# Banded attention and a feed-forward layer on one core: block sums of W1 built by adding DMA transfers instead of GpSimd additions

## The chip, the cores and the metric

The kernel runs on one core of a Trainium2 chip. The metric is the device time of one execution in microseconds (us); the median of several executions is compared. The engines of the core are TensorE (PE, its weight loads on a queue of their own, PEld), VectorE (DVE), ScalarE (ACT), GpSimd (POOL) and SyncE (SP). Each takes its instructions in the order of the program. DMA transfers are issued by SP, by POOL and, in one place, by ACT.

## What is computed

Attention over 4 batches and 8 heads (768 tokens, head dimension 64), in which a token sees the first 8 tokens and the 96 latest, with a bias that falls linearly with the distance; its output, 3072 tokens of 512 numbers, goes through a feed-forward layer. All in float32, but the two weight matrices arrive as float64:

```
scores = q @ k.T / 8 - slope[head] * dist,  -1e9 where not kept
a      = softmax(scores);   x = a @ v            # 3072 x 512
h      = x @ w_in                                # 512 -> 2048
out    = maximum(0.01 * h, h) @ w_out            # 2048 -> 512
```

## The kernel before

**Products.** Each float32 operand is split in a high part (rounded by a cast) and a low part (the rest), and each product is three matmuls: high by high, high by low, low by high. So a tile of the hidden layer (`hidden`, L1028: 128 hidden features by 384 tokens, four blocks of the 512 inputs) is 12 matmuls of 384 columns, and its way back to 512 outputs for 128 tokens (`project`, L1054) is 3 matmuls of 512 columns.

**Stages.** (1) Up to about 48 us the first attention units run while W1 (`wih`, `wil`) and W2 (`woh`, `wol`) are loaded and converted from float64. (2) A main loop of 96 steps `j` treats 2304 tokens in six chunks of 384: a step is one `hidden` (`ffn1(j)`) and three `project` (`ffn2(j - 1)`). The rest of the attention is hung between steps in "visits" (`visit`, L425; the steps at which they come are the list `VISITS`): a visit finishes two units (`attn_v` needs the tile `vr`, which SP has loaded; L310 to L338), starts two others, and issues loads for later ones. Results for the last 768 tokens are stored by POOL to a DRAM tensor `xd` (L356). (3) The last 768 tokens are done by `strassen` (L609), a Strassen-Winograd scheme with 7 instead of 8 block products: 8 iterations `i` with two of the 16 blocks of 128 hidden features each.

**The last phase.** An iteration has seven `product`s (six matmuls of 384 columns, L616), with blocks a11, a12, a22 of W1 or with one of four sums s1 to s4 of its blocks as weights, and as moving operand blocks of x (b11, b21, b22) or sums of them (t1 to t4). Between the products stand the 12 `project`s of the iteration before (`second`, L650; `todo` and `behind_` deal them out); in i = 0 there are only the three of the last main-loop step. DVE adds the products up (`add`, L636 to L638: u2, u3, c22, c21, c12), and `halves` (L626 to L634) makes the leaky maximum (L631, DVE), the cast (L632, ACT) and the low part (L633, DVE). `put` (L641 to L646) copies a finished output bank (L644) and stores it (L646, tensor `out_dram`); all six copies share three buffers with the tag "kept".

**Its operands.** `make_sums(i)` (L531 to L544) forms s1 to s4 of iteration i by ten POOL additions of 128x256 (high and low parts each), one iteration ahead; `split_sum` (L546 to L550) splits them with a cast on ACT and a subtraction on DVE. The differences of x (`diff`, L519 to L522, 128x768) are on POOL too: d1 gives t1, d2 t2, d4 t4, d3 t3. They are split by `split_x` (L514 to L517). `prepare(n)` (L566) hangs the loads of b (from `xd`, by POOL, L512), the differences and the splits at steps 12 to 1 before the end of the main loop. The split of b22 and the one of s4 for i = 0 come inside iteration 0.

The order of the instructions on each engine is the program's order as written; `pin` keeps it.

Of the kernel before, what the change touches and what calls it, by code (L numbers as in the profile page):

```python
# [18 lines left out]
P = 128  # L19
# [3 lines left out]
PAIRS = 22  # L23
HT = 384
SUPER = 2 * HT // P
VISITS = [39, 42, 46, 49, 53, 56, 60, 63, 67, 70, 74, 77, 81, 84, 88]
# [25 lines left out]
def fast_path(ctx, tc, qp, kp, vp, wi, wo, nvec, weights, nmall, out, B, H, S):  # L52
# [59 lines left out]
    def conversion(p):  # L112

        m, f = pieces[p]
        dh, dl = ((wih[:, :, f * P:(f + 1) * P], wil[:, :, f * P:(f + 1) * P]), (woh[:, f, :], wol[:, f, :]))[m]
# [383 lines left out]
    late, here = {}, {}  # L499
# [19 lines left out]
    def diff(name, in0, in1):  # L519
        t = pools["mem"].tile([P, 2, HT], F32, tag="diff", name="diff", bufs=2)  # L520
        pin(nc.gpsimd.tensor_tensor(out=t, in0=value(in0), in1=value(in1), op=ALU.subtract))
        late[name] = t  # L522

    def block(n, f, m):
        return [weights[x][:, 2 * m:2 * m + 2, f * P:(f + 1) * P] for x in range(2)]
# [4 lines left out]

    def make_sums(i):  # L531

        if i >= NF // 2:
            return
        b = blocks_of(i)
        a11, a12, a21, a22 = ([x.bitcast(F32) for x in b[k]] for k in ("a11", "a12", "a21", "a22"))
        for k, *terms in (("s1", a21[0], (ALU.add, a22[0]), (ALU.add, a21[1]), (ALU.add, a22[1])),
                          ("s2", here["s1"], (ALU.subtract, a11[0]), (ALU.subtract, a11[1])),
                          ("s3", a11[0], (ALU.subtract, a21[0]), (ALU.add, a11[1]), (ALU.subtract, a21[1])),
                          ("s4", a12[0], (ALU.subtract, here["s2"]), (ALU.add, a12[1]))):  # L540
            acc_ = terms[0]
            for op, t in terms[1:]:
                pin(nc.gpsimd.tensor_tensor(out=here[k], in0=acc_, in1=t, op=op))  # L543
                acc_ = here[k]  # L544

    def split_sum(i, k):  # L546
        if i >= NF // 2:
            return
        pin(nc.scalar.copy(out=late[k][0], in_=here[k]))
        pin(nc.vector.tensor_tensor(out=late[k][1], in0=here[k], in1=late[k][0].bitcast(F32), op=ALU.subtract))  # L550
# [15 lines left out]
    def prepare(n):  # L566
# [6 lines left out]
        elif n == -8:  # L573
# [8 lines left out]
            for k in ("s1", "s2", "s3", "s4"):  # L582
                late[k] = [mem.tile([P, 2, P], F32R, name=k + x) for x in "hl"]
                here[k] = mem.tile([P, 2, P], F32, name=k)
            make_sums(0)
            diff("d1", "b12", "b11")
            band_holds(tc, fl, nvec, nmall)
        elif n == -7:
            band_holds_everywhere(tc, fl, pools["ps"].tile([P, HT], F32, tag="ps_p", name="ps_f")[0:1, 0:1], flag)
        elif n == -6:  # L590
            split_sum(0, "s2")
            split_sum(0, "s3")
        elif n == -5:
            split_sum(0, "s1")
            split_x("b11")
        elif n == -4:
            diff("d2", "b22", "d1")
            split_x("t1", late["d1"])
        elif n == -3:
            split_x("t2", late["d2"])  # L600
            diff("d4", "d2", "b21")
        elif n == -2:
            split_x("t4", late["d4"])
            diff("d3", "b22", "b12")
            split_x("b21")
        elif n == -1:
            split_x("t3", late["d3"])

    def strassen():  # L609
# [26 lines left out]
        def add(name, in0, ps, op=ALU.add):  # L636
            t = in0 if name is None else ffn.tile([P, HT], F32, name="t") if name == "t" else mem.tile([P, HT], F32, name=name)
            pin(nc.vector.tensor_tensor(out=t, in0=in0, in1=ps, op=op))  # L638
# [498 lines left out]
```

## Time and profile before

| | us |
|---|---|
| median of 3 runs (lowest, highest) | 646.83 (646.46, 649.41) |
| the profiled execution | 644.86 |
| its span in the trace | 643.3 |
| PE busy | 621.2 (97%) |
| DVE busy | 424.6 (66%) |
| ACT busy | 291.4 (45%) |
| POOL busy | 119.5 (19%) |

The span runs from the first to the last instruction that the profiler saw; the execution's own time is 1.56 us longer. The table of windows among the rows below says how busy each engine was in a stretch of the span and is the place to look for idle time of PE. In the timelines a bracket behind an instruction says how long its engine had been idle ahead of it and what it waited for. The page's matmuls overlap: a matmul is shown for 0.34 or 0.40 us though the next starts sooner, so lost time is read from start to start.

### The profile page before, as it was taken

What the parts mean: (1) busy time and instruction counts of PE and PEld (TensorE: products, weight loads), DVE (VectorE), ACT (ScalarE), POOL (GpSimd) and SP (SyncE); (2) the same over time, 40 slices, a digit from 0 to 9 for tenths busy, and PEclk for the clock granted to TensorE, in tenths of its full rate; (3) what the DMA queues carried; (4) which work ended last, traced back from release to release, by engine and by line L of the source; (5) the groups of instructions that cost most, each with busy time, mean ns of one, the idle gap of its engine ahead of it and who ended that gap; (6) DMA issues with size and microseconds to landing.
All of it is one profiled execution on the core that took longest, in us unless ns stands there. A gap on an engine that the chain in (4) does not pass through costs nothing. (4 is left out here: it accounts for less than half of the span.)

```text
span 643.3 us, 14742 instructions
## 1 busy us (share of the span) xinstructions
PE 621.2 (97%) x5692; PEld 546.9 (85%) x5692; DVE 424.6 (66%) x1187; ACT 291.4 (45%) x822; POOL 119.5 (19%) x155
## 2 busy tenths in 40 slices
PE   5699999999999999999999999999999999999996
PEld 4588898898888888888888888898889878888885
DVE  6988998896667466575756566666227875555643
ACT  6977764545443344454434354445223532222212
POOL 3213300000000000000010020000145765555400
PEclk9899999999999999999999999999999999999999
DMA  8976743413667335376565666665620000000002
GB/s 275 355 269 217 224 153 132 142 55 120 220 202 242 107 112 185 123 230 199 187 183 180 225 208 196 212 225 184 182 66 1 26 25 1 2 1 0 2 1 102
DMA packets 56669, 92.79 MB, mean 144 GB/s; under 512 B 10144, under 2 KB 30688, under 8 KB 56592
## 3 DMA queue, kind: packets, MB, share of 16 engines
q1 hardware_dynamic: 54944, 86.79, 41.3%
q0 software_dynamic: 1504, 4.72, 2.4%
q8 instruction: 47, 0.77, 0.5%
q14 instruction: 30, 0.25, 0.1%
q10 hardware_dynamic: 144, 0.26, 0.1%
HBM read 70.26 MB, written 21.50 MB: 143 GB/s over the span
## 5 line engine op out<-in xcount | busy, mean ns | idle before, releaser
L1060 PE MATMUL ps_o<-woh,gl 128*128 128x512 f32 x336 | 133.3, 397 | 0.1
L1037 PE MATMUL ps_h<-xh,wih 128*128 128x384 f32 x384 | 132.8, 346 | 0.1
L1058 PE MATMUL ps_o<-woh,gh 128*128 128x512 f32 x336 | 132.4, 394 | 0.2
L1059 PE MATMUL ps_o<-wol,gh 128*128 128x512 f32 x336 | 132.3, 394 | 0.0
L1039 PE MATMUL ps_h<-xh,wil 128*128 128x384 f32 x384 | 129.4, 337 | 0.0
L1038 PE MATMUL ps_h<-xl,wih 128*128 128x384 f32 x384 | 129.3, 337 | 0.0
L1041 ACT COPY t<-ps_h 128x384 f32<-128x384 f32 x96 | 45.7, 476 | 121.4 <-PE ps_h L1039 121.3
L1042 DVE SCALAR_TENSOR_TENSOR t<-t 128x384 f32<-128x384 f32 x96 | 59.3, 618 | 59.5 <-ACT t L1041 57.8
L222 ACT ACTIVATE pr<-pr,nmall 128x192 f32<-128x192 f32 (+1 forms) x192 | 83.5, 438 | 6.3 <-DVE nmall L207 5.8
L356 POOL DMA_DIRECT2D xd<-xo x18 | 13.3, 740 | 374.1 <-ACT xo L355 374.0
L1037 PEld LDWEIGHTS ps_h<-xh,wih 128*128 128x128 f32 x384 | 72.0, 188 | 9.2 <-issue 2.0
L1048 DVE TENSOR_TENSOR gl<-t,gh 128x384 fp32r<-128x384 f32 x96 | 54.4, 567 | 36.0 <-ACT gh L1047 36.0
L1060 PEld LDWEIGHTS ps_o<-woh,gl 128*128 128x128 f32 x336 | 63.1, 188 | 15.7 <-DVE gl L1048 1.0
L1038 PEld LDWEIGHTS ps_h<-xl,wih 128*128 128x128 f32 x384 | 72.1, 188 | 2.9
L1039 PEld LDWEIGHTS ps_h<-xh,wil 128*128 128x128 f32 x384 | 72.1, 188 | 0.1
L1058 PEld LDWEIGHTS ps_o<-woh,gh 128*128 128x128 f32 x336 | 63.1, 188 | 10.1 <-ACT gh L1047 0.8
L1059 PEld LDWEIGHTS ps_o<-wol,gh 128*128 128x128 f32 x336 | 63.1, 188 | 10.0
L1047 ACT CAST gh<-t 128x384 fp32r<-128x384 f32 x96 | 49.1, 511 | 48.9 <-DVE t L1042 48.1
L543 POOL TENSOR_TENSOR s<-s,wil 128x256 f32<-128x256 f32 x48 | 43.6, 909 | 3.8
L207 DVE CUSTOM_DVE_ANT_0 pr<-ps_v,nbw 128x192 f32<-128x192 f32 x88 | 25.5, 354 | 27.5 <-ACT xo L355 12.8
L222 ACT ACTIVATION_READ_ACCUMULATOR pr<-pr,nmall 128x1 f32 x192 | 36.3, 189 | 0.0
L249 DVE TENSOR_SCALAR pr<-pr,rs 128x192 f32<-128x192 f32 (+1 forms) x136 | 33.7, 312 | 1.0
(184 smaller groups left out, 923.8 us busy)
## 6 DMA issues: line engine op xcount, KB each, us to landing
kr<-in_kp_dram SPq DMA_DIRECT2D x40, 384.0 KB, 4.6
vr<-in_vp_dram SPq DMA_DIRECT2D x40, 320.0 KB, 5.2
via<-pr SPq DMA_DIRECT2D x30, 384.0 KB, 2.8
pt<-via SPq DMA_DIRECT2D x120, 96.0 KB, 2.4
wst<-in_wi_dram SPq DMA_DIRECT2D x16, 512.0 KB, 3.8
wst<-in_wo_dram SPq DMA_DIRECT2D x16, 512.0 KB, 4.1
qs<-in_qp_dram SPq DMA_DIRECT2D x24, 256.0 KB, 4.3
out_dram<-part SPq DMA_DIRECT2D x20, 256.0 KB, 2.3
```

The source lines that it names most:

```text
L222: pin(nc.scalar.activation(out=p, in_=p, func=AF.Exp, scale=-1.0, bias=nm[:, 2 * a + j:2 * a + j + 1], accum_out=sm[:, 2 * a + j:2 * a + j ...
L543: pin(nc.gpsimd.tensor_tensor(out=here[k], in0=acc_, in1=t, op=op))
L1037: tc.keep_in_program_order(nc.tensor.matmul(ps, lhsT=wih[:, k, fs], rhs=xh[:, k, :CT], start=(k == 0), stop=False))
L1038: tc.keep_in_program_order(nc.tensor.matmul(ps, lhsT=wih[:, k, fs], rhs=xl[:, k, :CT], start=False, stop=False))
L1039: tc.keep_in_program_order(nc.tensor.matmul(ps, lhsT=wil[:, k, fs], rhs=xh[:, k, :CT], start=False, stop=(k == NK - 1)))
L1041: pin(copy(out=t, in_=ps))
L1042: pin(nc.vector.scalar_tensor_tensor(out=t, in0=t, scalar=0.01, in1=t, op0=ALU.mult, op1=ALU.max))
L1047: pin(copy(out=gh, in_=t))
L1048: pin(nc.vector.tensor_tensor(out=gl, in0=t, in1=gh.bitcast(F32), op=ALU.subtract))
L1058: tc.keep_in_program_order(nc.tensor.matmul(o, lhsT=gh[:, ts_], rhs=woh[:, f, :], start=first, stop=False))
L1059: tc.keep_in_program_order(nc.tensor.matmul(o, lhsT=gh[:, ts_], rhs=wol[:, f, :], start=False, stop=False))
L1060: tc.keep_in_program_order(nc.tensor.matmul(o, lhsT=gl[:, ts_], rhs=woh[:, f, :], start=False, stop=last))
```

## The change

- **Sums.** The 80 POOL additions are gone. A DRAM tensor `sd` of 128x2048 for each of s1 to s4 holds the sums for all eight iterations. It is filled by 14 steps, each a DMA issued by POOL: four are plain copies with which a sum begins (s1 and s3 from W1 in SBUF, s2 from s1 and s4 from s2 within DRAM), and ten add a block of W1 onto what is there (`accum_op=ALU.add`). Each step is done twice, for the columns of iterations 0 to 3 (512 KB) and for those of 4 to 7 (512 KB). The first half is done at the visits, one step each (two at the first), behind a POOL copy of one number that visit's DVE work writes (`few` from `nmall`); the second half is done in one go at step 88.
- **Loads.** `make_sums(i)` is now four SP loads of 128x256 from `sd`, two iterations ahead; two buffers.
- **Signs.** All sums are additions now; u2, u3 and c12 become subtractions, t3 comes from b12 - b22, and b22 is negated when it is split.
- **Layout.** W1 lies as [128, 2, 2, 8, 2, 128], so that a block of iterations is contiguous; `w1_of` picks tiles. Matmuls and conversions are the same in number.
- **Differences** are subtractions by DVE, one a step, in one buffer. The split of b22 and that of s4 for i = 0 move ahead of iteration 0, the last visit moves from step 88 to 87, the loads of b12 and b22 and the new pools one step earlier.
- **Order in the last phase.** `halves(c12)` is done in the next iteration, behind the copy of u1 (`rest`); in the last iteration `halves(c21)` comes sooner. Outputs 3 to 5 of `put` have buffers of their own; the flag is read ahead of the last 12 projections.

The core of the diff:

```diff
-VISITS = [39, 42, 46, 49, 53, 56, 60, 63, 67, 70, 74, 77, 81, 84, 88]
+VISITS = [39, 42, 46, 49, 53, 56, 60, 63, 67, 70, 74, 77, 81, 84, 87]
+def w1_of(w, f, m=None):
+    w = w[:, f % 2, :, f // 2]
+    return w.rearrange("p m k c -> p m (k c)") if m is None else w[:, m]
...
     def diff(name, in0, in1):
-        t = pools["mem"].tile([P, 2, HT], F32, tag="diff", name="diff", bufs=2)
-        pin(nc.gpsimd.tensor_tensor(out=t, in0=value(in0), in1=value(in1), op=ALU.subtract))
+        t = pools["mem"].tile([P, 2, HT], F32, tag="diff", name="diff", bufs=1) if name == "d1" else late["d1"]
+        pin(nc.vector.tensor_tensor(out=t, in0=value(in0), in1=value(in1), op=ALU.subtract))
...
+    def sum_step(n, batch):
+        k, r, m, x, other = (("s1", 1, 0, 0, None), ("s3", 0, 0, 0, None), ("s1", 1, 1, 0, 0), ("s3", 1, 0, 0, 0),
+                             ("s1", 1, 0, 1, 0), ("s3", 0, 0, 1, 0), ("s1", 1, 1, 1, 0), ("s3", 1, 0, 1, 0),
+                             ("s2", 0, 0, 0, "s1"), ("s2", 0, 0, 0, 0), ("s2", 0, 0, 1, 0),
+                             ("s4", 0, 0, 0, "s2"), ("s4", 0, 1, 0, 0), ("s4", 0, 1, 1, 0))[n]
+        cols = slice(2 * P * batch.start, 2 * P * batch.stop)
+        to, of = sd[k][:, cols], sd[other][:, cols] if isinstance(other, str) else wide[x][:, r, m, cols]
+        pin(nc.gpsimd.dma_start(out=to, in_=of, **(dict(accum_op=ALU.add) if other == 0 else {})))
...
     def make_sums(i):
-        for k, *terms in (("s1", a21[0], (ALU.add, a22[0]), (ALU.add, a21[1]), (ALU.add, a22[1])),
-                          ("s2", here["s1"], (ALU.subtract, a11[0]), (ALU.subtract, a11[1])),
-                          ("s3", a11[0], (ALU.subtract, a21[0]), (ALU.add, a11[1]), (ALU.subtract, a21[1])),
-                          ("s4", a12[0], (ALU.subtract, here["s2"]), (ALU.add, a12[1]))):
-            acc_ = terms[0]
-            for op, t in terms[1:]:
-                pin(nc.gpsimd.tensor_tensor(out=here[k], in0=acc_, in1=t, op=op))
-                acc_ = here[k]
+        t = pools["mem"].tile([P, 4, 2 * P], F32, name="sums", bufs=2)
+        for n, k in enumerate(("s1", "s2", "s3", "s4")):
+            pin(nc.sync.dma_start(out=t[:, n], in_=sd[k][:, 2 * P * i:2 * P * (i + 1)]))
...
     def prepare(n):
-        elif n == -8:
+        elif n == -9:
...
             make_sums(0)
-            diff("d1", "b12", "b11")
...
+        elif n == -6:
+            diff("d1", "b12", "b11")
+            split_x("b11")
         elif n == -5:
-            split_sum(0, "s1")
-            split_x("b11")
+            split_x("t1", late["d1"])
+            diff("d2", "b22", "d1")
...
         elif n == -1:
-            split_x("t3", late["d3"])
+            hi, lo = late["b22"]
+            pin(nc.scalar.activation(out=hi, in_=lo.bitcast(F32), func=AF.Copy, scale=-1.0))
+            pin(nc.vector.scalar_tensor_tensor(out=lo, in0=lo.bitcast(F32), scalar=-1.0, in1=hi.bitcast(F32), op0=ALU.mult,
+                                               op1=ALU.subtract))
+            split_sum(0, "s4")
...
         def put(tt, bank):
-            ob = outs.tile([P, DM], F32, tag="kept", name="part", bufs=CHUNKS[0])
+            ob = (outs.tile([P, DM], F32, tag="kept", name="part", bufs=CHUNKS[0]) if tt < 3
+                  else mem.tile([P, DM], F32, tag=("t2h", "t3h", "t1h")[tt - 3], name="part"))
...
             product(b["a11"], "b11", ps)
+            make_sums(i + 2)
             u1 = mem.tile([P, HT], F32, name="u1")
             pin(nc.scalar.copy(out=u1, in_=ps))
-            split_sum(i, "s4")
-            make_sums(i + 1)
+            rest()
+            if i:
+                split_sum(i, "s4")
...
-            if i == 0:
-                split_x("b22")
...
-            c12 = add(None, u2, ps)
-            gs[1, 0] = halves(c21)
-            gs[0, 1] = halves(c12)
+            c12 = add(u2, u2, ps, ALU.subtract)
+            if i < NP - 1:
+                gs[1, 0] = halves(c21)
+            rest = lambda gs=gs, c12=c12: gs.update({(0, 1): halves(c12)})
...
+        if j in VISITS:
+            n = VISITS.index(j)
+            u = PAIRS + 2 * n
+            if u < NUNIT:
+                pin(nc.gpsimd.tensor_copy(out=few[:, 6:7], in_=nmall[:, 4 * u:4 * u + 1]))
+                for x in range(n + (n > 0), n + 2):
+                    sum_step(x, range(0, NP // 2))
+        if j == len(order) - 8:
+            for x in range(STEPS):
+                sum_step(x, range(NP // 2, NP))
```

How this stands on the engines. VectorE around the end of the main loop, before: the last steps' leaky maximum and low part (t, gl), the splits of t4, b21 (`b_6011`), t3 and s4, then iteration 0, with u2 (`u_6493`), u3 (`u_6528`), c22 (t), and the split of b22 between them.

```order
934 L1042 SCALAR_TENSOR_TENSOR t<-t 128x384
935 L1048 TENSOR_TENSOR gl<-t,gh 128x384
936 L517 TENSOR_TENSOR t3l<-diff,t3h 128x768
937 L550 TENSOR_TENSOR s4l<-s_6209,s4h 128x256
938 L638 TENSOR_TENSOR u_6493<-u_6472,ps_p 128x384
939 L550 TENSOR_TENSOR s2l<-s_6203,s2h 128x256
940 L631 SCALAR_TENSOR_TENSOR t<-t 128x384
941 L492 COPY part<-ps_o 128x512
942 L638 TENSOR_TENSOR u_6528<-u_6472,ps_p 128x384
943 L633 TENSOR_TENSOR gl<-t,gh 128x384
944 L550 TENSOR_TENSOR s3l<-s_6206,s3h 128x256
945 L517 TENSOR_TENSOR b22l<-b22l,b22h 128x768
```

The same place in the changed kernel, from the step with the last difference on.

```order
933 L523 TENSOR_TENSOR t4l<-diff,t4h 128x768
934 L527 TENSOR_TENSOR diff<-t3l,b22l 128x768
935 L1078 SCALAR_TENSOR_TENSOR t<-t 128x384
936 L1084 TENSOR_TENSOR gl<-t,gh 128x384
937 L523 TENSOR_TENSOR t3l<-diff,t3h 128x768
938 L523 TENSOR_TENSOR b_6042<-b_6042 128x768
939 L1078 SCALAR_TENSOR_TENSOR t<-t 128x384
940 L1084 TENSOR_TENSOR gl<-t,gh 128x384
941 L628 SCALAR_TENSOR_TENSOR b22l<-b22l,b22h 128x768
942 L567 TENSOR_TENSOR s4l<-sums,s4h 128x256
943 L660 TENSOR_TENSOR u_6528<-u_6519,ps_p 128x384
944 L567 TENSOR_TENSOR s2l<-sums,s2h 128x256
```

The differences have come in, and the splits of t3 and b22 now stand ahead of the last step's low part and of iteration 0.

GpSimd from the loads of the last blocks of x on, before: sums for i = 0, then the four differences, then the sums for i = 1.

```order
28 L356 DMA xd<-xo 128x2x128 x2
29 L512 DMA t3l<-xd 128x2x384
30 L512 DMA b22l<-xd 128x2x384
31 L543 TENSOR_TENSOR s_6200<-wih 128x256
...
38 L543 TENSOR_TENSOR s_6209<-s_6209,wil 128x256
39 L521 TENSOR_TENSOR diff<-t3l,b_6009 128x768
40 L521 TENSOR_TENSOR diff<-b22l,diff 128x768
41 L521 TENSOR_TENSOR diff<-diff,b_6011 128x768
42 L521 TENSOR_TENSOR diff<-b22l,t3l 128x768
```

The same in the changed kernel: the second half of the sums (`sum_s_115` is s1's DRAM tensor, 116 that of s2, 117 of s3, 118 of s4).

```order
61 L362 DMA xd<-xo 128x2x128 x2
62 L518 DMA t3l<-xd 128x2x384
63 L518 DMA b22l<-xd 128x2x384
64 L549 DMA sum_s_115<-wih 128x1024
65 L549 DMA sum_s_117<-wih 128x1024
66 L549 DMA sum_s_115<-wih 128x1024
67 L549 DMA sum_s_117<-wih 128x1024
...
75 L549 DMA sum_s_118<-sum_s_116 128x1024
76 L549 DMA sum_s_118<-wih 128x1024
77 L549 DMA sum_s_118<-wil 128x1024
```

After these GpSimd has no work left in the fast path but the reading of the flag.

## Rows read from the trace of the kernel before

**Rows 1.** Windows of the span: window, its length, then busy us (and instructions) of PE, PEld, DVE, ACT and POOL, the granted clock of PE, the busy share of the DMA engines, and GB/s.

```profile
130.00:462.00 332.00, 332.00 (x3200) 293.46 (x3199) 209.05 (x696) 149.03 (x464) 14.08 (x19) 1.00 0.57 180
462.00:506.00 44.00, 44.00 (x293) 39.36 (x292) 23.09 (x29) 14.85 (x30) 22.00 (x21) 1.00 0.13 40
506.00:526.00 20.00, 18.32 (x92) 15.95 (x91) 17.32 (x27) 8.56 (x19) 16.57 (x18) 1.00 0.11 41
526.00:637.50 111.50, 111.45 (x546) 98.97 (x544) 62.28 (x115) 29.47 (x66) 44.58 (x51) 1.00 0.02 8
```

**Rows 2.** PE's timeline in iterations 0 and 1 of the last phase: start, duration (us), engine, line, operation, tiles, shape, and in brackets the idle time ahead and what ended it.

```profile
510.80 0.40 PE L1060 MATMUL ps_o<-woh,gl 128*128 128x512 f32 x1
511.42 0.44 PE L620 MATMUL ps_p<-t3h,s3h 128*128 128x384 f32 x1 [0.22 <-DVE u L638]
...
515.02 0.34 PE L620 MATMUL ps_p<-t4l,wih 128*128 128x384 f32 x1
515.19 0.34 PE L620 MATMUL ps_p<-t4h,wil 128*128 128x384 f32 x1
516.43 0.42 PE L620 MATMUL ps_p<-b22h,s4h 128*128 128x384 f32 x1 [0.90 <-DVE t L638]
...
522.00 0.40 PE L1059 MATMUL ps_o<-wol,gh 128*128 128x512 f32 x1
522.24 0.40 PE L1060 MATMUL ps_o<-woh,gl 128*128 128x512 f32 x1
523.20 0.62 PE L620 MATMUL ps_p<-b,wih 128*128 128x384 f32 x2 [0.56 <-ACT u L687]
```

**Rows 3.** DVE's timeline in the same stretch.

```profile
511.70 1.08 DVE L631 SCALAR_TENSOR_TENSOR t<-t 128x384 f32<-128x384 f32 x1
...
513.31 0.54 DVE L638 TENSOR_TENSOR u<-u,ps_p 128x384 f32<-128x384 f32 x1
...
514.88 0.95 DVE L517 TENSOR_TENSOR b22l<-b22l,b22h 128x768 fp32r<-128x768 f32 x1
515.74 0.54 DVE L638 TENSOR_TENSOR t<-u,ps_p 128x384 f32<-128x384 f32 x1
...
521.12 1.10 DVE L631 SCALAR_TENSOR_TENSOR u<-u 128x384 f32<-128x384 f32 x1
```

**Rows 4.** ACT's timeline in iterations 1 and 3.

```profile
522.25 0.51 ACT L632 CAST gh<-u 128x384 fp32r<-128x384 f32 x1 [1.64 <-DVE u L631]
522.67 0.47 ACT L687 COPY u<-ps_p 128x384 f32<-128x384 f32 x1
523.04 0.41 ACT L549 CAST s4h<-s 128x256 fp32r<-128x256 f32 x1
...
554.17 0.41 ACT L549 CAST s4h<-s 128x256 fp32r<-128x256 f32 x1
```

**Rows 5.** Groups of DVE's instructions by line and form, first in 506 to 526 us, then in 610 to 637 us, where POOL has nothing left to do: line, operation, tiles, shape, count, busy us and mean ns of one, idle time ahead.

```profile
L631 DVE SCALAR_TENSOR_TENSOR t<-t 128x384 f32<-128x384 f32 x3 | 2.9, 983 | 0.0
...
L631 DVE SCALAR_TENSOR_TENSOR t<-t 128x384 f32<-128x384 f32 x3 | 1.7, 554 | 2.1 <-ACT t L698 2.1
```

**Rows 6.** Groups by line and form: a split of 128x768 on DVE in 480 to 506 us, and a difference of 128x768 on POOL in 462 to 640 us.

```profile
L517 DVE TENSOR_TENSOR t2l<-diff,t2h 128x768 fp32r<-128x768 f32 x1 | 1.0, 960 | 0.2 <-ACT t2h L516 0.2
...
L521 POOL TENSOR_TENSOR diff<-t3l,b 128x768 f32<-128x768 f32 x1 | 2.0, 2034 | 0.0
```

**Rows 7.** All engines' timeline at the end of the span.

```profile
637.05 0.40 PE L1060 MATMUL ps_o<-woh,gl 128*128 128x512 f32 x1
638.18 0.69 DVE L644 COPY part<-ps_o 128x512 f32<-128x512 f32 x1 [1.35 <-PEq L1074]
638.90 0.37 ACTq L646 DMA_DIRECT2D out_dram<-part  x1
```

**Rows 8.** Stores of the last phase, time from issue to landing, one store each: the first (issued at 632.5 us), the third (633.9) and the last (638.9).

```profile
DMA to landing us min/median/max: 2.0/2.0/2.0
...
DMA to landing us min/median/max: 4.2/4.2/4.2
...
DMA to landing us min/median/max: 3.1/3.1/3.1
```

**Rows 9.** DMA issues: tiles, queue, count, KB of each, median us from issue to landing.

```profile
wst<-in_wo_dram SPq DMA_DIRECT2D x16, 512.0 KB, 4.1
...
xl<-xd POOLq DMA_DIRECT2D x1, 768.0 KB, 6.0
```

**Rows 10.** POOL's timeline at one of the visits (two stores of x).

```profile
439.81 1.46 POOL L356 DMA_DIRECT2D xd<-xo  x2 [18.38 <-ACT xo L355]
```

**Rows 11.** PE's timeline at the first matmul of two visits, the last but four and the last.

```profile
401.14 0.43 PE L326 MATMUL ps_v<-pt,vr 64*64 64x128 f32 x5
...
470.87 0.34 PE L326 MATMUL ps_v<-pt,vr 64*64 64x128 f32 x4
```

**Rows 12.** Loads of `vr` by SP for these two visits (two transfers each): first and last start, and time to landing.

```profile
L175 SPq DMA_DIRECT2D vr<-in_vp_dram x2: 424/424/424, 391.2 to 391.6; - x2
...
DMA to landing us min/median/max: 6.1/6.2/6.4
...
L175 SPq DMA_DIRECT2D vr<-in_vp_dram x2: 429/430/432, 457.8 to 458.3; - x2
...
DMA to landing us min/median/max: 7.8/8.0/8.2
```

More of the change, by code (lines that the diff above doesn't have):

```diff
@@ L496, in ffn2 @@
             nc.sync.dma_start(out=out[r0:r0 + P, :], in_=ob)
-    late, here = {}, {}
+    late, sums_of = {}, {}
     def side(k, x):
@@ L548, in split_sum @@
             return
-        pin(nc.scalar.copy(out=late[k][0], in_=here[k]))
-        pin(nc.vector.tensor_tensor(out=late[k][1], in0=here[k], in1=late[k][0].bitcast(F32), op=ALU.subtract))
+        pin(nc.scalar.copy(out=late[k][0], in_=sums_of[i][k]))
+        pin(nc.vector.tensor_tensor(out=late[k][1], in0=sums_of[i][k], in1=late[k][0].bitcast(F32), op=ALU.subtract))
     def reload(n):
@@ L678, in strassen @@
             if i == NF // 2:
+                rest()
+                flags.append(nc.values_load(flag, min_val=0, max_val=1,
+                                            skip_runtime_bounds_check_because="the flag is a comparison's result"))
                 behind_(12)
@@ L692, in strassen @@
             product(late["s2"], "t2", ps2)
-            u2 = add("u2", u1, ps2)
+            u2 = add(mem.tile([P, HT], F32, name="u2"), u1, ps2, ALU.subtract)
             split_sum(i + 1, "s2")
@@ L701, in strassen @@
             product(late["s3"], "t3", ps2, first=False)
[L702 removed]
+            u3 = add(mem.tile([P, HT], F32, name="u3"), ps2, u1, ALU.subtract)
             split_sum(i + 1, "s3")
[L704 to L705 removed]
             behind_(2 if i else 1)
@@ L708, in strassen @@
             product(late["s1"], "t1", ps)
-            c22 = add("t", u3, ps)
+            c22 = add(ffn.tile([P, HT], F32, name="t"), u3, ps)
             split_sum(i + 1, "s1")
@@ L713, in strassen @@
             product(b["a22"], "t4", ps2)
-            c21 = add(None, u3, ps2, ALU.subtract)
+            c21 = add(u3, u3, ps2, ALU.subtract)
+            if i == NP - 1:
+                gs[1, 0] = halves(c21)
             gs[1, 1] = halves(c22)
@@ L717, in strassen @@
             product(late["s4"], "b22", ps, first=False)
-            c12 = add(None, u2, ps)
-            gs[1, 0] = halves(c21)
-            gs[0, 1] = halves(c12)
+            c12 = add(u2, u2, ps, ALU.subtract)
+            if i < NP - 1:
+                gs[1, 0] = halves(c21)
+            rest = lambda gs=gs, c12=c12: gs.update({(0, 1): halves(c12)})
             behind_(12)
@@ L1002, in general_ffn @@
     wih, wil, woh, wol = weights
-    NK, NF, DM = wih.shape[1], woh.shape[1], woh.shape[2]
+    NK, NF, DM = 2 * wih.shape[2], woh.shape[1], woh.shape[2]
     CT = xs.shape[-1]
@@ L1031, in hidden @@
     wih, wil = weights[:2]
-    NK = wih.shape[1]
+    NK = 2 * wih.shape[2]
     copy = copy or nc.scalar.copy
-    fs = slice(f * P, (f + 1) * P)
     ps = psum.tile([P, CT], F32, tag="ps_h", name="ps_h")
+    wih, wil = ([w1_of(w, f, m)[:, k] for m in range(2) for k in range(2)] for w in (wih, wil))
     for k in range(NK):
-        tc.keep_in_program_order(nc.tensor.matmul(ps, lhsT=wih[:, k, fs], rhs=xh[:, k, :CT], start=(k == 0), stop=False))
-        tc.keep_in_program_order(nc.tensor.matmul(ps, lhsT=wih[:, k, fs], rhs=xl[:, k, :CT], start=False, stop=False))
-        tc.keep_in_program_order(nc.tensor.matmul(ps, lhsT=wil[:, k, fs], rhs=xh[:, k, :CT], start=False, stop=(k == NK - 1)))
+        tc.keep_in_program_order(nc.tensor.matmul(ps, lhsT=wih[k], rhs=xh[:, k, :CT], start=(k == 0), stop=False))
+        tc.keep_in_program_order(nc.tensor.matmul(ps, lhsT=wih[k], rhs=xl[:, k, :CT], start=False, stop=False))
+        tc.keep_in_program_order(nc.tensor.matmul(ps, lhsT=wil[k], rhs=xh[:, k, :CT], start=False, stop=(k == NK - 1)))
     t = pool.tile([P, CT], F32, name="t")
```

46 lines of the change are left out of this document (23 added, 23 removed).

## Prediction

> **What bounds the kernel now.** I read the windows of the span first, to see where TensorE stands still: it is busy 332.00 of 332.00 us in the main loop, 44.00 of 44.00 behind it, and 111.45 of 111.50 from 526 us on, at a granted clock of 1.00, the upper level of 2.4 GHz, in each [rows 1]. So nothing that only frees GpSimd or VectorE in these stretches can shorten the kernel. Only 506 to 526 us, iterations 0 and 1 of the last phase, has a gap: 18.32 of 20. The second view is TensorE's timeline there. From start to start a matmul of 384 columns takes 0.17 (515.02 to 515.19) and one of 512 columns 0.24 (522.00 to 522.24) when nothing is in the way. Three starts are late [rows 2]: the first s3 matmul 511.42 - 510.80 - 0.24 = 0.38, the first s4 matmul 516.43 - 515.19 - 0.17 = 1.07, the first of a12 in iteration 1 523.20 - 522.24 - 0.24 = 0.72. Sum **2.17 us**. The brackets say who was late: VectorE's u3 sum (tile u), its c22 sum (tile t), ScalarE's copy of u1.
>
> The third view says why. VectorE is busy 17.32 of these 20 us and GpSimd 16.57 [rows 1]. Ahead of the c22 sum at 515.74 VectorE does the split of b22 (0.95 us), and earlier a leaky maximum of 1.08 us [rows 3]. The same maximum takes 983 ns on average here and 554 ns where GpSimd is done [rows 5]: 0.43 us more per instruction beside GpSimd's additions. In iteration 1 the c12 maximum at 521.12 takes 1.10; behind it stands ScalarE's cast (522.25), and behind that the copy of u1 (522.67), for which TensorE waits [rows 3, 4]. So the wait is a queue on ScalarE that begins with a stretched instruction on VectorE.
>
> The last view is the end of the span. The last matmul ends by 637.05 + 0.40 = 637.45, but the copy of its bank starts at 638.18 [rows 7]. The page puts that idle time on a TensorE instruction which is not in the copy's way. The copy's buffer is that of the third store, issued at 633.9 and landed 4.2 us later, at 638.1 [rows 8]: there is the releaser. The first store took 2.0, so this is a late landing, not a law.
>
> **The change part by part.**
>
> *GpSimd's additions go.* VectorE's instructions fall towards their length at 610 us. In 506 to 526 there are three maxima at 983 instead of 554 (1.3 us saved), and the split of b22 (0.95) leaves. Both stalls that VectorE made are shorter than that: 0.38 and 1.07. The order of the c22 sum, the copy of u1 and `halves(c12)` also changes so that the copy comes first, which takes the third stall by itself. I cost the remaining stall at 0: -2.17. Next late behind it would be c21 and the s4 product in iteration 0, which has only three projections and so the least cover; a walk through VectorE's queue with the lengths of 610 us leaves it ready by some tenths of a us. If that cover is gone, up to 0.4 comes back.
>
> *Four differences and the negated split of b22 come to VectorE* in the last six steps. A difference of 128x768 took 2.03 on GpSimd; on VectorE its nearest row is a split of the same shape, 0.96 [rows 6]. Four make 3.9, b22's about 1.1 (twice the 554 of a 128x384 maximum) and s4's split was there before. A step lasts 12 x 0.17 + 9 x 0.24 = 4.2 us; VectorE was busy 23.09 of the 44 us [rows 1], about half, so each step has 2 us free and takes 1 more. Hidden: 0. If a difference took 2.0 here too, the queue would fill a step exactly, and a few tenths would show.
>
> *28 adding transfers.* Their issue is GpSimd's only work; ahead of a visit's stores it had been idle 18.38 us [rows 10]. No row shows an adding transfer. Below, one of 512 KB costs what a plain one does, 4.1 us to landing; above, twice that, 8.2, as the destination is read and written too; 768 KB from GpSimd took 6.0 [rows 9]. I take 5, nearest to the plain ones. The half at the visits has a visit's spacing for one transfer, so its own length is no matter; that it disturbs other transfers is rival C. The other half starts at about 473: the last visit starts a step earlier, 470.87 - 4.2 = 466.7 [rows 11], and some 6 us go to its stores and the two loads of x (an estimate from 1.46 us for two issues and one landing). Ten rounds follow each other (s1 and s3 side by side four times, then three for s2 and three for s4): 473 + 50 = 523. They are first needed in iteration 4: its s4 cast, two iterations of (554.17 - 523.04) / 2 = 15.6 each at 523.04 and 554.17, falls at 569.7, in the changed order near 566 [rows 4]; less 3 for the load, 563. Cover 40 us: 0.
>
> *32 loads by SyncE* at 0.43 us of issue each [rows 12]: SyncE has nothing else from the last visit on but stores, and loads stand two iterations ahead. 0. *Moving the last visit* one step forward: its `vr` was issued at 458.3 and landed 8.2 later, at 466.5, and is used at 466.7 now instead of 470.87 [rows 11, 12]. 0.2 us are left; 0 to 0.5 may be lost here. The new layout of W1 changes no count of instructions: 0.
>
> *Own buffers for the last outputs.* The last copy starts when the matmul is done, about 0.06 behind 637.45: 638.18 - 637.51 = **-0.67**. The last store's landing (3.1) I leave.
>
> Sum on the profiled execution: 644.86 - 2.17 - 0.67 + 0 (up to 0.5 for the last visit, 0.4 for iteration 0) = 642.0. The median of the runs lies 1.97 above that execution, and I take the difference over: 646.83 - 2.84 = **644.0**.
>
> **The rivals.** *A, a quicker end.* The last store landed in 3.1 where the first took 2.0 [rows 8]. If the load on the transfers that made 4.2 and 3.1 is a matter of the moment, the changed kernel may get 2.0: another -1.1, 642.9. For it: two of three landings differ without a change of size. Against: the same end of program follows.
>
> *B, the stalls stay.* VectorE carries more now, and if its long instructions were long by themselves and not through GpSimd, iteration 0 starts with a queue and the waits move to the same places; then only the end is gained: 646.2. Against: 983 and 554 for the same instruction [rows 5].
>
> *C, slower: adding transfers delay `vr`.* The main loop keeps the DMA engines at a share of 0.57 [rows 1], and the visit at 401.14 gets its `vr` at 391.6 + 6.4 = 398.0: 3.1 us early [rows 11, 12]. An adding transfer issued in the same stretch, holding the load back by x, costs x - 3.1 at such a visit. With three visits as tight as this (an upper guess): no loss to 3.1, the gain of 2.84 eaten at x = 4.1, slower by 0.5% from x = 5.2, and at 5.7, 644.0 + 7.8 = 651.8. For it: the load for the last visit took 8.2 instead of 6.4 without any such transfer. Against: a whole plain 512 KB is landed in 4.1, and loads and sums share the engines rather than queue behind each other. The Trainium skill ("DMA: Bandwidth & Descriptors", section "Issuing engines are not separate DMA queues") says that transfers issued by different engines end up on the same 16 DMA engines and interleave; so GpSimd's queue is no shelter for SyncE's loads, which speaks for C in kind and, by the interleaving, against x being the whole transfer. By that rule, the trace agrees as far as it goes (the main loop's share is one figure for all queues).
>
> *D, slower: the second half comes late.* Ten rounds in 90 us (473 to 563) leave 9 us for each. At 10 us a round s4 lands 10 us late, some 2 of which ScalarE's queue covers: 652. At 12 us, 672. For it: nothing bounds an adding transfer but my two rows. Against: even twice the plain transfer, 8.2, is in time. The Trainium skill ("SBUF — State Buffer", section "SBUF: two separate sides") warns that a transfer issued by GpSimd can sit without descriptors while VectorE holds the port they share. By that rule, a round would wait up to the longest VectorE instruction of the rows, 1.1 us: 10 rounds end at 534 instead of 523, still in time, but with 8.2 it would be 9.3 and late, so I put D at 0.09 instead of 0.06. No row here shows such a wait.
>
> **How the numbers follow.** Forecast 0.50, A 0.15, B 0.13, C 0.13, D 0.09. What a measurement of this kernel can tell from no change is about 0.5%, 3.2 us: faster means under 643.6, slower over 650.1. The forecast lies just inside; of its 0.50 I put 0.19 under 643.6 (less at the end, as in part of A) and 0.31 above. A gives 0.14 to faster and 0.01 to same, B 0.13 to same, C 0.06 to same and 0.07 to slower, D 0.09 to slower. Together faster 0.33, same 0.51, slower 0.16. The range leaves out D, the upper half of C and a little below A: 642.2 to 649.0.
>
> **What would show it.** In the windows of the changed kernel TensorE has no gap over 0.2 us between 506 and 526, and the three waits of rows 2 are gone; the maximum there takes about 0.55. If it is still 0.98, B's reason holds. The last copy starts within 0.1 us of the last matmul's end. GpSimd's transfers show their landing: about 5 us each at the end of the main loop, the last before 530; over 9 us is D. At the visits, a gap ahead of `attn_v` with `vr` as its releaser is C; a gap at the last visit alone is the moved step. I am wrong, above all, if new waits appear in 130 to 506 us, where TensorE has had none.

## The result: slower, by transfers that keep a store waiting

| | us |
|---|---|
| before, median of 4 runs (lowest, highest) | 646.64 (644.99, 649.41) |
| changed, median of 4 runs (lowest, highest) | 652.16 (650.64, 652.84) |
| ratio, 95% interval | 1.0084 (1.0057 to 1.0111) |
| changed, the profiled execution, its span | 652.84, 651.3 |

The change costs 0.84%. The windows of the changed kernel show where (columns as in [rows 1]):

```profile
130.00:462.00 332.00, 326.74 (x3095) 286.83 (x3098) 207.31 (x695) 146.91 (x458) 24.51 (x42) 0.99 0.67 196
462.00:506.00 44.00, 44.00 (x364) 39.59 (x357) 17.42 (x30) 13.77 (x29) 11.19 (x15) 1.00 0.75 188
506.00:526.00 20.00, 20.00 (x104) 18.49 (x103) 13.71 (x23) 10.05 (x20) 3.13 (x4) 1.00 0.82 174
526.00:645.00 119.00, 118.55 (x581) 105.28 (x579) 60.90 (x125) 33.04 (x73) 2.28 (x3) 1.00 0.19 47
```

Beside [rows 1]: the gap of 506 to 526 us is closed (20.00 of 20 instead of 18.32), and a new one of 5.26 us has come in the main loop, which had none. The last window's 0.45 is only its end, behind the last matmul. All waits of TensorE from 100 us on in the changed kernel (engine, tile and line, waited for what, us in total, times, longest):

```profile
PE ps_o L1094 <- ACT gh L1083: 3.9, 1, 3.9
PE ps_v L332 <- issue: 0.7, 1, 0.7
PE ps_av L332 <- DMA pt<-via: 0.4, 1, 0.4
PE ps_v L332 <- DMA vr<-in_vp_dram: 0.2, 1, 0.2
```

One wait of 3.9 us carries it. The timeline of all engines of the changed kernel around it (start, duration, engine, line, what, idle time ahead and its releaser), cut to the rows of the chain:

```profile
389.38 0.98 POOL L549 DMA_DIRECT2D sum_s<-wil  x1
...
389.64 0.38 SPq L238 DMA_DIRECT2D via<-pr  x1
...
395.77 0.36 DVE L213 CUSTOM_DVE_ANT_0 pr<-ps_v,nbw 128x192 f32<-128x192 f32 x1 [7.11 <-DMA via<-pr]
...
396.17 0.46 ACT L228 ACTIVATE pr<-pr,nmall 128x192 f32<-128x192 f32 x1 [5.66 <-DVE nmall L213]
...
396.88 0.56 DVE L1078 SCALAR_TENSOR_TENSOR t<-t 128x384 f32<-128x384 f32 x1
...
397.48 0.51 ACT L1083 CAST gh<-t 128x384 fp32r<-128x384 f32 x1 [0.32 <-DVE t L1078]
...
398.04 0.80 PE L1094 MATMUL ps_o<-woh,gh 128*128 128x512 f32 x1 [3.88 <-ACT gh L1083]
```

Read it from the bottom. TensorE waits for the cast gh of the feed-forward layer. ScalarE had idled 5.66 us on the visit's softmax and VectorE 7.11 us on the buffer `pr` of an attention unit, because the store `via<-pr` that reads it (SyncE writes `pr` to a DRAM tensor `via`, and the tile `pt` is loaded from there) had not landed; the leaky maximum of the feed-forward layer (L1078) stood behind that on VectorE, although ScalarE had written its input by 390.51. The store was issued 0.26 us behind an adding transfer. Its time from issue to landing, in the view of that one transfer:

```profile
DMA to landing us min/median/max: 6.0/6.0/6.0
```

The chain begins one store earlier. Of SyncE's rows ahead of it, and the landing of the first of them:

```profile
379.10 0.33 SPq L238 DMA_DIRECT2D via<-pr  x1
386.48 3.07 SPq L240 DMA_DIRECT2D pt<-via  x4
...
DMA to landing us min/median/max: 7.4/7.4/7.4
```

The store at 389.64 was ready at 382.99, when VectorE had written its `pr`; but SyncE takes its work in order and stood at the loads of `pt`, which need the store of 379.10 to have landed (379.10 + 7.4 = 386.5). That earlier store went out 5.6 us behind an adding transfer that took 6.9 us to land, and beside a 768 KB load of `xl` by GpSimd that the kernel before has there too. In the kernel before the same two stores took 5.2 and 4.3 us, and VectorE's wait at this place was shorter:

```profile
383.55 0.38 SPq L232 DMA_DIRECT2D via<-pr  x1
...
388.03 0.36 DVE L207 CUSTOM_DVE_ANT_0 pr<-ps_v,nbw 128x192 f32<-128x192 f32 x1 [2.77 <-DMA via<-pr]
```

So the wait grew by 4.3 us: 1.7 of it is the later store's own landing, and the rest its late start, in which the 2.2 us more of the earlier store stand.

The stop has a second price. The windows around it (same columns):

```profile
394.00:398.00 4.00, 0.15 (x1) 0.00 (x0) 1.67 (x9) 1.51 (x6) 0.00 (x0) 0.94 0.52 117
398.00:401.00 3.00, 2.96 (x7) 2.38 (x8) 2.88 (x9) 1.24 (x5) 0.00 (x0) 0.52 0.87 294
401.00:405.00 4.00, 4.00 (x21) 3.61 (x21) 3.32 (x10) 0.99 (x2) 0.00 (x0) 1.00 0.94 309
```

TensorE was busy 0.15 of 4 us; in the next 3 us its granted clock is 0.52, the lower level of 1.2 GHz, and the next 512-column matmuls start 0.59 and then five times 0.43 us apart instead of 0.23. From start to start the wait costs 4.05 us and the clock 1.3.

The rest of the profiled difference: the visit at 385.27 began 0.9 us late, with its `vr` landing as it began, and the one at 461.64 0.4. The 2.17 us of waits [rows 2] are gone. The stretch ahead of the first visit ended 1.9 us later, but that varies from profile to profile (227.6 to 231.9 us over the twelve, and 228.4 to 231.9 over the five whose programs are the same up to there: changed, e1, e2, e5 and e10), so the table of experiments gives the time from the first visit's first matmul to the last matmul's start.

### The profile page after: what moved, and what is told of

The parts are those of the page before. It is cut to its first block, busy times and chain, and to the rows that moved or that the text cites. A ratio compares the mean times of both kernels' runs of the same rounds, so it can differ in the third digit from the quotient of the medians.

```text
span 651.3 us, 14774 instructions
## 1 busy us (share of the span) xinstructions
PE 624.3 (96%) x5692; PEld 548.8 (84%) x5692; DVE 410.7 (63%) x1191; ACT 293.2 (45%) x822; POOL 63.4 (10%) x112
## 4 chain that ended last, share of the span: by engine, by line
PE 82%; DVE 5%; DMA 5%; ACT 3%; issue 1%; POOL 1%; SPq 1%; POOLq 0%; DVEq 0%; ACTq 0%
PE ps_o L1096 11%; PE ps_o L1094 10%; PE ps_o L1095 10%; PE ps_h L1073 10%; PE ps_p L643 9%; PE ps_h L1075 9%; PE ps_h L1074 9%; DMA via<-pr 3%; PE ps_v L199 2%; PE ps_v L344 2%; PE ps_q L1096 2%; PE ps_q L1094 2%; PE ps_q L1095 2%; DMA vr<-in_vp_dram 2%; PE ps_v L332 1%
## 5 line engine op out<-in xcount | busy, mean ns | idle before, releaser
L1078 DVE SCALAR_TENSOR_TENSOR t<-t 128x384 f32<-128x384 f32 x96 | 55.4, 577 | 53.3 <-ACT t L1077 52.2
L258 DVE STREAM_TRANSPOSE pr<-pr 128x768 f32<-128x768 f32 (+1 forms) x34 | 32.1, 945 | 0.9
```

What stands on the lines that cost most here:

```text
L1078: pin(nc.vector.scalar_tensor_tensor(out=t, in0=t, scalar=0.01, in1=t, op0=ALU.mult, op1=ALU.max))
```

## The experiments

In the order of the runs. T1 is the reading above; T2 the rival that the loss comes from another new thing in the main loop. The times are medians; a ratio is to the kernel before, with its 95% interval. "First visit to last matmul" is 409.5 us before and 414.6 in the changed kernel.

**e1_quarter_adds.** The ten adding steps of the first half with a quarter of their columns.

```diff
-                    sum_step(x, range(0, NP // 2))
+                    sum_step(x, range(0, NP // 2) if x in (0, 1, 8, 11) else range(0, 1))
```

> The changed kernel with the ten adding transfers of the first half cut to a quarter of their columns (128 KB instead of 512 KB; the sums of iterations 1 to 3 are left incomplete by it; the four plain copies, the issues and the waits stay). Theory T1, the transfers at the visits hold up SyncE's stores and loads, a store of pr keeps its buffer, and VectorE, ScalarE and TensorE wait behind it in turn: the wait of 3.9 us near 398 us and the lowered clock behind it are gone or under 1 us, 644 to 647 us. Theory T2, the loss comes from something else that is new in the main loop (layout of W1, the GpSimd copy that waits for nmall, the moved visit): the wait stays, 650 to 653 us.

644.58 us, ratio 0.9970 (0.9951 to 0.9990). TensorE waits nowhere in the main loop; first visit to last matmul 407.2. T2 falls: the layout, the GpSimd copy and the moved visit are all still there.

**e2_twice_traffic.** One more plain 512 KB at each of the 13 visits that have a step of the sums.

```diff
+                pin(nc.gpsimd.dma_start(out=spare[n], in_=wide[0][:, 0, 0, :4 * 2 * P]))
```

> The changed kernel with one more plain transfer of 512 KB (W1 to an unused DRAM tensor) behind the adding one at each visit. T1: several visits stall, each by some us, with a store of pr or a load of vr or pt as releaser; 657 to 675 us. T2: no visit stalls more than now, 651 to 653 us.

663.92 us, ratio 1.0268 (1.0241 to 1.0296). Waits at several visits, as T1 said:

```profile
PE ps_o L1096 <- ACT gh L1085: 4.6, 3, 4.1
PE ps_v L332 <- issue: 4.2, 2, 3.6
PE ps_v L332 <- DMA vr<-in_vp_dram: 2.8, 2, 1.6
```

**e3_early_half.** The first half in one go at step 24, none at the visits.

```diff
-        if j in VISITS:
-            n = VISITS.index(j)
...
+        if j == 24:
+            for x in range(STEPS):
+                sum_step(x, range(0, NP // 2))
```

> The changed kernel with the first half's 14 transfers in a row once W1 is converted (step 24 of the program), ahead of the visits, and none at the visits. T1: no wait near 398 us; the 14 transfers last some 70 us and fall in 130 to 215 us, where TensorE had no gap; 643 to 646 us, more if the attention units of that stretch have as little slack as the visits. T2: 650 to 653 us.

644.14 us, ratio 0.9951 (0.9933 to 0.9969), in the range that T1 gave. The transfers ran from 85 to about 156 us, sooner than I had said: the first began once its piece of W1 was converted (the loads of the two weight matrices last to some 130 us, not to 48 as the part on stages above has it). SyncE stores no `pr` between 80 and 160 us, so there was no attention unit that could have paid. The DMA engines were busier there than at the changed kernel's visits, 0.84 of the time beside 0.72 (0.38 in this stretch of the kernel before), and TensorE's busy time is the same as before, 70.70 of 71 us:

```profile
85.00:156.00 71.00, 70.70 (x406) 62.58 (x405) 60.03 (x112) 38.24 (x78) 10.38 (x13) 1.00 0.84 209
```

From 100 us to the end the view of waits lists none for TensorE; first visit to last matmul 406.9. This version beats both kernels.

**e4_pool_sums.** No adding transfer at all: ten GpSimd additions per iteration again, the rest as changed.

```diff
-            pin(nc.sync.dma_start(out=t[:, n], in_=sd[k][:, 2 * P * i:2 * P * (i + 1)]))
...
+                pin(nc.gpsimd.tensor_tensor(out=t[:, n], in0=got, in1=x, op=ALU.add))
...
-                    sum_step(x, range(0, NP // 2))
...
-                sum_step(x, range(NP // 2, NP))
```

> The changed kernel without any adding transfer: the sums are made by ten GpSimd additions per iteration as before, two iterations ahead, all else as changed (layout, differences on VectorE, order of the last phase, own output buffers). T1: no wait in the main loop; TensorE's three waits of 506 to 526 us are gone or under 0.5 us in all though GpSimd adds there, since VectorE has less to do; 643 to 646 us. T2: 648 to 653 us. A third reading, that GpSimd's additions alone made the waits of iterations 0 and 1: these waits are back with 1 to 2 us, 645 to 647 us.

644.33 us, ratio 0.9963 (0.9947 to 0.9980). The waits of iterations 0 and 1 do not come back, though GpSimd adds beside VectorE there; the third reading falls. Its windows, the last of them around iteration 0, first in the kernel before and then in e4:

```profile
462.00:506.00 44.00, 43.77 (x290) 38.78 (x289) 25.00 (x34) 15.45 (x31) 20.93 (x24) 1.00 0.16 48
506.00:526.00 20.00, 20.00 (x104) 18.25 (x103) 15.51 (x27) 9.61 (x21) 10.95 (x13) 1.00 0.11 41
...
509.00:517.00 8.00, 6.88 (x35) 5.81 (x35) 8.00 (x13) 4.06 (x10) 5.27 (x7) 1.00 0.25 99
...
509.00:517.00 8.00, 8.00 (x44) 7.44 (x43) 6.31 (x12) 4.47 (x10) 5.82 (x7) 1.00 0.24 93
```

GpSimd is busy with additions in these 8 us as long as before (5.82 and 5.27 us); what fell is VectorE's work, from 8.00 to 6.31.

A small wait stands at 494 us (0.40 from start to start), in a step in which VectorE does a difference and GpSimd adds. So the sums by transfer (e3) buy 0.8 us over GpSimd's additions (e4) in the profiles, 406.9 and 407.8 from first visit to last matmul, and nothing that the medians tell apart (644.14 and 644.33).

**e5_in_three_pieces.** Each step of the first half cut into 128, 128 and 256 KB at three successive steps.

```diff
+        for back, cols in enumerate((range(0, 1), range(1, 2), range(2, NP // 2))):
+            if j - back in VISITS:
...
+                    pin(nc.gpsimd.tensor_copy(out=few[:, 6:7], in_=gts[j][0][:, 0:1].bitcast(F32)))
```

> The changed kernel with each 512 KB step of the first half cut into three transfers (128, 128 and 256 KB) at three successive steps of the main loop, each released by that step's work. All bytes as in the changed kernel. If it is a burst of 512 KB beside SyncE's store that hurts (T1a): no wait over 1 us in the main loop, 644 to 647 us. If the bytes in a visit's interval are too many wherever they fall (T1b): waits of some us, perhaps at other visits, 649 to 655 us.

659.28 us, ratio 1.0195 (1.0164 to 1.0226): worse than whole, and past T1b's bound. The waits are of the same kind (three on gh, 6.7 us in all, behind stores of pr). A 128 KB transfer of `wil`, all of them adding, takes 6.2 us to land at the median, nearly as long as one of 512 KB (6.4); one of `wih`, a third of them plain, 3.2. Now some transfer is about in every step. That T1a falls is clear; why pieces are that much worse is not, since this kernel also has more GpSimd copies and reads of gh.

**e6_splits_ahead** and **e7_c12_later** take the parts of the change that have nothing to do with the sums and put them into the kernel before. First e6:

```diff
+        elif n == -1:
+            split_x("b22")
+            split_sum(0, "s4")
...
-            split_sum(i, "s4")
+            if i:
+                split_sum(i, "s4")
```

> The kernel before with one part of the change: the four differences on VectorE, one a step, and the splits of b22 and s4 ahead of iteration 0. GpSimd's additions stay as they were. If VectorE's work inside iteration 0 made the first two waits: the waits at s3 and s4 (0.38 and 1.07 us) are gone and the one at a12 in iteration 1 (0.72) stays; 645 to 646 us beside 646.9. If GpSimd's additions made them by themselves: all three stay within a third, 646 to 647.

645.72 us, ratio 0.9995 (0.9979 to 1.0011). The waits at s3 and s4 are gone, the one at a12 stays, as expected, but two new ones have come at 498 and 499 us (0.47 and 0.59 from start to start), where VectorE's differences stand beside GpSimd's additions. All TensorE waits from 480 us on:

```profile
PE ps_p L622 <- ACT u L689: 0.5, 1, 0.5
PE ps_o L1061 <- DVE gl L1049: 0.4, 1, 0.4
PE ps_o L1059 <- ACT gh L1048: 0.3, 1, 0.3
```

So e6 gains nothing that can be told from the kernel before. Nor does it keep the two readings apart as it was meant to: without the differences GpSimd got through its additions sooner, and from 509 to 517 us it is busy 1.54 us instead of 5.27:

```profile
509.00:517.00 8.00, 8.00 (x44) 7.51 (x43) 5.99 (x12) 5.12 (x11) 1.54 (x2) 1.00 0.17 67
```

Then e7:

```diff
+            rest()
             split_sum(i, "s4")
...
-            gs[0, 1] = halves(c12)
+            rest = lambda gs=gs, c12=c12: gs.update({(0, 1): halves(c12)})
...
+            ob = (outs.tile([P, DM], F32, tag="kept", name="part", bufs=CHUNKS[0]) if tt < 3
+                  else mem.tile([P, DM], F32, tag=("t2h", "t3h", "t1h")[tt - 3], name="part"))
```

> The kernel before with two other parts of the change: halves(c12) behind the copy of u1 of the next iteration, and own buffers for the last three outputs. The wait of 0.72 us at a12 in iteration 1 is gone, those at s3 and s4 stay; the last copy starts within 0.1 us of the last matmul's end (0.7 sooner); 645 to 646.3 us beside 646.9. If the wait in iteration 1 hangs on the late start of iteration 0's end, it stays.

644.80 us, ratio 0.9975 (0.9958 to 0.9991). The wait at a12 is gone, the other two stay (0.9 and 0.2 in that view), and the last copy follows the last matmul (which ends at 637.08) by 0.03:

```profile
636.68 0.40 PE L1063 MATMUL ps_o<-woh,gl 128*128 128x512 f32 x1
...
637.11 0.69 DVE L645 COPY part<-ps_o 128x512 f32<-128x512 f32 x1 [0.71 <-PE ps_o L1063]
```

**e8_plain_transfers** and **e9_plain_double**: e4 with a transfer at each visit that adds nothing, of 512 KB and of 1 MB.

```diff
+                    pin(nc.gpsimd.dma_start(out=spare[x], in_=wide[0][:, 0, 0, :4 * 2 * P]))
```

> The changed kernel with GpSimd's additions in place of the sums in DRAM (as in e4_pool_sums), and at each visit one plain transfer of 512 KB to an unused DRAM tensor, at the place and with the release of the adding one. If 512 KB of any kind at this place hurt: a wait of some us in the main loop as in the changed kernel, 649 to 653 us. If adding makes the price (the destination is read as well): no wait over 1 us, 644 to 647 us.

644.58 us, ratio 0.9974 (0.9954 to 0.9994): beside e4's 644.33, plain transfers of the same bytes cost nothing that can be told. That left two readings, and e9 was made for them.

```diff
-                    pin(nc.gpsimd.dma_start(out=spare[x], in_=wide[0][:, 0, 0, :4 * 2 * P]))
+                    pin(nc.gpsimd.dma_start(out=spare[x], in_=wide[0][:, 0, 0]))
```

> As e8_plain_transfers, with one plain transfer of 1 MB at each visit instead of 512 KB. Worked out from the shares of GpSimd's queue, an adding transfer of 512 KB holds the 16 engines for about 2.9 us together (14.6% of 651 us less 2.4% of 643, over 28), a plain one for 1.4; so 1 MB plain is the adding one's weight without adding. If it is the weight on the engines (T-load): the same kind of stall, a store of pr late, VectorE waiting for it 10 us or more in all between 220 and 480 us, DMA share there about 0.72, 648 to 655 us. If adding does something of its own (T-add): no wait over 1 us, 643 to 646.5 us.

653.36 us, ratio 1.0086 (1.0053 to 1.0119), the changed kernel's ratio without a single adding transfer. T-load holds, T-add falls: weight alone is enough for the harm. That adding does nothing of its own beside it is not shown. Its waits of TensorE:

```profile
PE ps_o L1098 <- ACT gh L1087: 4.3, 2, 2.8
PE ps_v L332 <- issue: 1.3, 1, 1.3
```

**e10_half_adds.** As e1, with half the columns instead of a quarter.

```diff
-                    sum_step(x, range(0, NP // 2) if x in (0, 1, 8, 11) else range(0, 1))
+                    sum_step(x, range(0, NP // 2) if x in (0, 1, 8, 11) else range(0, 2))
```

> As e1_quarter_adds, with the ten adding transfers of the first half at half their columns (256 KB; the sums of iterations 2 and 3 are left incomplete). T-load: between e1 and the changed kernel, VectorE's wait for stores of pr 5 to 17 us, TensorE waits 0 to 2 us, 644 to 648 us. T-add: the number of adding transfers is the same as in the changed kernel, so a stall of 2 us or more stays, 648 to 652 us.

648.93 us, ratio 1.0032 (1.0008 to 1.0056), between e1 and the changed kernel; its runs spread from 645.94 to 652.51. It tells less than hoped: the median lies in T-add's range, VectorE's wait (16.2 us) in T-load's, and the longest wait of TensorE is 1.0 us, too short for T-add, though its waits in the main loop add up to 2.6 us, more than T-load's 2. Half the bytes make nearly the changed kernel's wait on VectorE. The weight on the engines did fall: GpSimd's queue held them for 0.127 x 648.0 = 82.3 us, 12.8 less than in the changed kernel (95.1, worked out below), 1.3 for each of the ten halved transfers. So VectorE's wait does not follow the weight step by step.

**The doses together.** In each kernel: VectorE's wait for the store of `pr` in the window 220 to 480 us, the DMA engines' busy share there, the median landing of that store, and first visit to last matmul.

| kernel | wait (times), us | DMA share | store lands, us | first visit to last matmul, us |
|---|---|---|---|---|
| e3, none at visits | 0.3 (1) | 0.58 | 2.6 | 406.9 |
| before | 3.3 (2) | 0.57 | 2.8 | 409.5 |
| e8, plain 512 KB | 2.8 (2) | 0.65 | 2.8 | 408.0 |
| e1, adding 128 KB | 5.2 (2) | 0.65 | 2.7 | 407.2 |
| e10, adding 256 KB | 16.2 (5) | 0.69 | 3.7 | 410.9 |
| changed, adding 512 KB | 16.8 (6) | 0.72 | 4.2 | 414.6 |
| e9, plain 1 MB | 20.7 (6) | 0.71 | 4.1 | 416.8 |
| e2, adding and plain 512 KB | 24.7 (10) | 0.76 | 4.1 | 425.3 |
| e5, adding, in pieces | 25.0 (8) | 0.76 | 4.2 | 418.8 |

The rows behind two lines of it, VectorE's wait in the changed kernel, and in e9:

```profile
DVE pr L213 <- DMA via<-pr: 16.8, 6, 7.1
```

```profile
DVE pr L213 <- DMA via<-pr: 20.7, 6, 5.3
```

DMA queues and issues of the changed kernel (of a queue: packets, MB, share of 16 engines' span; of an issue: count, KB, median us to landing), and then of e8:

```profile
q0 software_dynamic: 5536, 19.40, 14.6%
...
via<-pr SPq DMA_DIRECT2D x30, 384.0 KB, 4.2
...
sum_s<-wih POOLq DMA_DIRECT2D x12, 512.0 KB, 6.6
sum_s<-wil POOLq DMA_DIRECT2D x12, 512.0 KB, 6.4
```

```profile
q0 software_dynamic: 3520, 12.06, 5.5%
...
via<-pr SPq DMA_DIRECT2D x30, 384.0 KB, 2.8
...
spare<-wih POOLq DMA_DIRECT2D x14, 512.0 KB, 5.3
```

GpSimd's own queue (q0) held the engines for 0.146 x 651.3 = 95.1 us in the changed kernel, 35.4 in e8 and 0.024 x 643.3 = 15.4 before. So a transfer of the changed kernel weighs (95.1 - 15.4) / 28 = 2.8 us, eight plain copies among them, and a plain one of e8 (35.4 - 15.4) / 14 = 1.4; the plain 1 MB of e9, with 0.081 x 653.3 = 52.9 us on that queue, weighs 2.7. It is not the bytes that decide: in the window of the table e8 moves 210 GB/s and loses nothing, the changed kernel 207.

In this stretch nothing is lost up to a share of 0.65; in the five kernels from 0.69 on the stores are late, and TensorE pays for the part of VectorE's wait that the step does not cover. Each line is one profile, so whether there is a step between 0.65 and 0.69 or a steep slope is not shown; and e3's share of 0.84 at 85 to 156 us cost nothing, with no store of `pr` there.

## Why the prediction was wrong, point by point

**What bounds the kernel, and the 2.17 us.** Right in size: with no disturbance at the visits, first visit to last matmul falls by 2.5 us in e3 and 2.3 in e1, and 506 to 526 us is full. e3's 644.14 is near the forecast of 644.0 for a kernel whose transfers are hidden, in part by luck: its last stretch, from the last matmul's end to the end of the span, takes 6.6 us instead of 5.9, where 0.67 less had been forecast. The reason is in part open. The third wait went by the order of c12 and u1 alone, as forecast (e7). For the first two the prediction named two causes together, the maxima stretched by GpSimd's additions and the split of b22 that stood in the way. The stretching was read rightly: the leaky maximum takes 555 to 558 ns in the changed kernel beside 983 before. But it was not needed for the cure: in e4 GpSimd adds beside iteration 0 as long as before, and with the splits gone from there neither wait is left. e6 took out the splits and most of these additions at once. No run takes only the additions out of the kernel before, so whether that would have been enough too is open. Where VectorE has the differences and GpSimd still adds, new waits stand at 494 to 505 us, from start to start 0.4 us in e4 and e9, 0.6 in e8 and 1.1 in e6, and in no kernel without the additions; removing them is what GpSimd's silence is worth. So rival B's fear, that VectorE carries too much, is seen only where GpSimd adds too.

**Differences on VectorE, loads by SyncE, the moved visit, the new layout.** Hidden, as forecast: a difference takes 0.95 us on VectorE beside 0.96 that I took; 462 to 506 us has no gap; the last visit loses under 0.15 us.

**Own output buffers: -0.67.** Shown for the copy (it starts 0.03 us behind the matmul, in e7 too). But the last store then took 3.7 us to land instead of 3.1, so rival A did not come, and the span of the changed kernel ends 2.3 us behind that landing instead of 1.3 (last section). From the last matmul's end to the end of the span it takes 6.75 us instead of 5.85: the term came out as +0.9.

**The step that failed** is the sentence on the adding transfers that "The half at the visits has a visit's spacing for one transfer, so its own length is no matter". This half was put at nothing, and it cost 7.7 us: first visit to last matmul takes 414.6 us in the changed kernel and 406.9 in e3, which has no transfer at the visits. The sentence looked at the transfer that was added and its own consumer. What decides is who else waits on the engines. Rival C did ask that, had the right mechanism in kind and the chance 0.13, but it looked at the load `vr` with its 3.1 us and found a break-even of 4.1 us of delay at three visits. `vr` cost 0.9 and 0.4 us in the changed kernel. The transfer with the least room was a store: `via<-pr` holds a buffer that VectorE needs at the next unit, the kernel before waited for it already (3.3 us in two waits), and two stores that took 5.2 and 4.3 us there and 7.4 and 6.0 in the changed kernel delay SyncE's queue too. The row of that wait was in the answers that I had asked for ahead of the prediction, for VectorE from 220 to 470 us (3.3 us, two times, longest 2.8) and is missing from the rows that I went by. The price of an adding transfer was undersized as well: I took 5 us and had 8.2 as the upper end; they land in 6.4 to 6.6 us at the median. Of the 28 transfers 20 add, and on the engines the mix weighs twice what a plain one does. The Trainium skill ("DMA: Bandwidth & Descriptors", section "Issuing engines are not separate DMA queues") had it: transfers of GpSimd and SyncE run on the same 16 engines. The trace agrees: the stores land in 4.2 us at the median beside the transfers, and in 2.8 without them.

**The second half (rival D)** did not decide. It began 11 us later than I had it and took 63 us instead of 50, 484 to 547 us; TensorE waits nowhere from 500 us on, so the 40 us of cover took both. The Trainium skill ("SBUF — State Buffer", section "SBUF: two separate sides") warns of descriptors that GpSimd cannot write while VectorE holds a shared port. No sign of it was seen, as far as the issuing instructions tell: GpSimd's for the sums took 0.55 to 0.98 us each. The section speaks of VectorE's two-port operations, not of every instruction as the prediction took it, and no row here tells them apart, so this is no test of it.

**Chances.** Slower by over 0.5% had 0.16, of which 0.07 was with the mechanism that came (C's chance of 0.13 was split, 0.06 to no change); the other 0.09 was D, which did not come.

## What to carry to other kernels

Before adding transfers that look free, list every transfer in that stretch whose landing releases an engine, stores that free a buffer included, and read from the waits of all engines how much room each has left; the tightest one sets the price, and one late buffer on an in-order engine stops work that has nothing to do with it. Look for a stretch in which those users have room or are not there: the same 14 transfers cost 7.7 us at the visits and nothing at 85 to 156 us. And take a change apart: the kernel without any adding transfer (e4, 644.33) gains as much as the best one with them (e3, 644.14), and reordering one copy with own output buffers (e7, 644.80) gives most of that by itself.

## What was unexpected

- The DMA engines' share is a poor warning: at the visits 0.65 was free and 0.69 to 0.72 was not, while 0.84 was free in e3's stretch without stores of `pr`.
- A stop of 3.9 us cost 1.3 us more by the granted clock, 0.52 for the next 3 us. In e9 a wait of 2.9 us from start to start had the same pace behind it (0.43 us from start to start for six matmuls), at a granted clock of 0.50 from 327 to 330 us.
- In each of the six kernels that hold the sums in DRAM (changed, e1, e2, e3, e5, e10) the span ends 2.3 to 2.6 us behind the landing of the last store; in the six others 1.3. The instructions there are the program's closing ones. VectorE's last but one starts 1.3 to 1.6 us behind the one ahead of it in the six with the sums in DRAM, and 0.1 us behind it in the six others. It takes some 1 us from the gain of e3; the cause is open and no run was made for it.
